# Sixteen small loads into an unread tile, set between the large loads of a one-core decode kernel

## The chip, the cores and the metric

One Trainium2 chip, one of its cores. The metric is the device time of one execution in microseconds; the kernel before has a median of 376.76 us over two runs (376.64 to 376.88). The profile is of one further execution of the same program, which took 376.91 us, of which 375.1 us lie between the first and the last recorded instruction.

## The reference

One token (a row `x` of 512 numbers) goes through a parallel block: attention over a cache of 4096 positions with 32 heads of 128, and beside it a gated feed-forward of width 1376. All is float32. Cut to what is computed:

```python
xn = layernorm(x)
q = (xn @ wq).reshape(1, 1, 32, 128).transpose(0, 2, 1, 3)
scores = einsum("bhqd,bhkd->bhqk", q, k_cache) * 128 ** -0.5
o = einsum("bhqk,bhkd->bhqd", softmax(scores), v_cache)
attn = o.transpose(0, 2, 1, 3).reshape(1, 1, 4096) @ wo
ffn = xn + ((silu(xn @ w_gate) * (xn @ w_up)) @ w_down) * sigmoid(xn @ w_r)
return x + attn + ffn
```

Two caches of 67.1 MB each and five weight matrices, about 159 MB in all, are read once from HBM and used once. (`silu` and `sigmoid` of the feed-forward act on one token; choosing the best of one token changes nothing.)

## The kernel before, in words

The 32 heads are worked in eight groups of four (`HP = 4`, `NG = 8`). For a group, `load_keys(g)` brings its keys as one load of 128 rows of 64 KB (8.39 MB) and `load_group(v_cache, g, ...)` its values as another load of that size; both are issued at line 102. Each row goes to one of the 128 partitions of the on-chip memory.

Two places hold these loads. `ring` has three slots of 32 KB a partition and some room behind; `vals` has two slots. The keys of group 0 go into `vals`, those of later groups into slots 0 and 1 or 1 and 2 of `ring` by turns; values go into `vals`, but those of the last group into `ring`. `wq` stands in the first two slots of `ring` at the start, `w_gate` and `w_up` in what lies behind them (four loads of 64 rows each, line 92, two for each matrix). At the end `w_down` (line 92, two loads) and `wo` (line 117, one load of 4096 KB and five of 2048, 1024, 640, 256 and 128 KB) go into places that have come free.

VectorE multiplies the keys with the query (line 250) and sums them (line 261); GpSimd takes a share of the rows (lines 266 and 268). TensorE forms the sum of the values with the softmax weights (line 338). A load into a place waits until the instructions that read the place before are done, and until the load that wrote it before has landed.

All these loads are issued by SyncE (rows of SPq) in the order of the program, and SyncE waits in that order too: an issue that must wait holds up all later ones. The order is `wq`, keys 0, `w_gate` twice, `w_up` twice, keys 1, values 0, keys 2, values 1 and so on to keys 7, values 6, values 7, `w_down`, `wo`. The rows `x` and `w_r` are issued by ScalarE. Loads that were issued stand in a queue at each of the 16 DMA engines, and an engine goes through its share of one after its share of the other. Eight semaphores serve the loads by turns to tell of landing; a load takes the semaphore of the load eight before it only once that one has landed.

After the last `wo` load, TensorE multiplies its rows (line 417), ScalarE and VectorE copy the row of results (lines 485 and 487), and SyncE stores it (line 488).

Of the kernel before, what the change touches and what calls it, by code (L numbers as in the profile page):

```python
# [8 lines left out]
F32 = mybir.dt.float32  # L9
# [4 lines left out]
P = 128  # L14
# [6 lines left out]
NCOL = 4  # L21
PARTS = (16,), (8, 4, 2.5, 1, 0.5)
T = 32


@with_exitstack
def kernel(
# [13 lines left out]
    nc = tc.nc  # L41
    _, H, Sk, Dh = k_cache.shape
# [26 lines left out]
    const = ctx.enter_context(tc.tile_pool(name="const", bufs=1))  # L69
# [12 lines left out]
    def load_wq(t):  # L82
        nc.sync.dma_start(t, wq.rearrange("(p j) n -> p (j n)", p=P))  # L83

        return [
            t[:, j * H * Dh:(j + 1) * H * Dh].rearrange("p (b h k n) -> p b h k n", b=NB, h=HP, n=QC)
            for j in range(NK)
        ]

    def halves(t, w):  # L90
        for i in range(2):
            nc.sync.dma_start(t[i::2], w[i::2])

    def load_in(t, w):
        halves(t, w.rearrange("(p j) f -> p (j f)", p=P))
        return [t[:, j * F:(j + 1) * F] for j in range(NK)]

    def load_group(cache, g, t, c0=0):

        n = t.shape[1]  # L100
        src = cache[0].rearrange("(b h g) (p c) d -> b g p h (c d)", b=NB, g=GB, p=PP)[g // GB, g % GB]
        nc.sync.dma_start(t, src[:, :, c0 * Dh:c0 * Dh + n])
        return t.rearrange("p (c d) -> p c d", d=Dh)

    def load_keys(g):

        i = (1 - g % 2) * SLOT
        t = load_group(k_cache, g, ring[:, i:i + 2 * SLOT] if g else vals)
        t = [t[:, :HC], t[:, HC:]]
        return [(h, t[h]) for h in ((1, 0) if g % 2 else (0, 1))]  # L110

    def load_wo(t, b, parts):
        src = wo[b * BH * Dh:(b + 1) * BH * Dh, :].rearrange("(p r) n -> p (r n)", p=P)
        x = 0
        for n in parts:
            y = x + int(n * D)
            nc.sync.dma_start(t[:, x:y], src[:, x:y])  # L117
            x = y
        return t.rearrange("p (r n) -> p r n", n=D)

    def load_down(t):
        halves(t, w_down.rearrange("f n -> (f n)").rearrange("(p x) -> p x", p=P))
        return t
# [4 lines left out]
    nc.scalar.dma_start(xr, x[0])  # L128
    nc.scalar.dma_start(wr, w_r.rearrange("(o n) -> o n", o=1))
    WQ = load_wq(ring[:, :2 * SLOT])  # L130
    K, V = {0: load_keys(0)}, {}


    ones = const.tile([P, P], F32, name="ones")
# [20 lines left out]

    own = const.tile([P, HP, T], F32, name="own")
    nc.vector.tensor_copy(own, mine[:, :, None].to_broadcast([P, HP, T]))

# [4 lines left out]

    first = const.tile([P, G, HP, T], F32, name="first")
    nc.gpsimd.memset(first, 0.0)
# [3 lines left out]
    for j in range(1, NCOL):  # L169
        nc.vector.tensor_tensor(sel, sel, rows_at[j], op=ALU.add)  # L170
    turned = const.tile([P, NCOL - 1 + T], F32, name="turned")
    nc.gpsimd.memset(turned, 0.0)
# [48 lines left out]
    for j in range(NK):  # L221
        for i in range(NQ * HP):
            t, k = i % NCOL, i // HP
            nc.tensor.matmul(ps_pv[i // NCOL][32 * t:32 * t + 1, :QC], xnT[:, j:j + 1],  # L224
                             WQ[j][:, k * QB // GB, i % HP, k % (GB // QB), :],
                             start=(j == 0), stop=(j == NK - 1), skip_group_check=True)
# [4 lines left out]

    behind = ring[:, 2 * SLOT:]
    W_GATE, W_UP = (load_in(behind[:, i * NK * F:(i + 1) * NK * F], w) for i, w in enumerate((w_gate, w_up)))
    late = [ring[:, SLOTS * SLOT + i * D:SLOTS * SLOT + (i + 1) * D] for i in range(MORE // D)]

    def q_part(k):

        ps = ps_q.tile([P, QB, Dh], F32, name="q")
        nc.tensor.matmul(ps.rearrange("p g d -> p (g d)"), pick.rearrange("p i h -> p (i h)"), q_sb[:, k, :],
                         start=True, stop=True)  # L240

        nc.scalar.activation(q_sb[:, k, :], ps.rearrange("p g d -> p (g d)"), AF.Copy)
        return ps
# [4 lines left out]
    def multiply(g, i, c0, c1):  # L248
        q, k = Q[g // QB][:, g % QB, :], K[g][i][1]
        nc.vector.tensor_tensor(  # L250
            k[:, c0:c1, :], k[:, c0:c1, :],
            q[:, None, :].to_broadcast([P, c1 - c0, Dh]), op=ALU.mult
        )

    def sums(g, i):
        if i == 0:
            S[g] = small.tile([P, C], F32, name="s")
        h, k = K[g][i]
        s = S[g][:, h * HC:(h + 1) * HC]
        for c, n in ((slice(0, HC - NP), Dh), (slice(HC - NP, HC), Dh // 2)):  # L260
            nc.vector.tensor_reduce(s[:, c], k[:, c, :n], axis=AX.X, op=ALU.add)  # L261

    def rest(g, i):

        k, q = K[g][i][1][:, HC - NP:], q_sb[:, g // QB, :].rearrange("p (g d) -> p g d", d=Dh)[:, g % QB, :]
        nc.gpsimd.tensor_tensor(k, k, q[:, None, :].to_broadcast([P, NP, Dh]), op=ALU.mult)  # L266
        a, b = k[:, :, :Dh // 2], k[:, :, Dh // 2:]
        nc.gpsimd.tensor_tensor(a, a, b, op=ALU.add)  # L268
# [17 lines left out]
    def ffn_hidden():  # L286

        hid = sigmoid(gate, [P, FT], "hid")
        nc.vector.tensor_tensor(hid, hid, gate, op=ALU.mult)
        hr = late[3][:, :(NS + 1) * T].rearrange("p (s i) -> p s i", i=T)  # L290
        nc.vector.memset(hr, 0.0)
        for a in range(HP):
# [5 lines left out]
            )  # L298
        hT = late[4][:, :(NS + 1) * T].rearrange("p (s i) -> p s i", i=T)
        nc.vector.transpose(hT.rearrange("p s i -> p (s i)"), hr.rearrange("p s i -> p (s i)"))  # L300
# [7 lines left out]
    def own_max(g):  # L308
        m = small.tile([P, 1], F32, name="m")
        nc.vector.reduce_max(m, S[g], axis=AX.X)  # L310
        dg = small.tile([P, PP], F32, name="dg")
        nc.vector.tensor_scalar(dg, fold, m, SCALE, op0=ALU.mult, op1=ALU.mult)  # L312
        ps = ps_s.tile([P, 512], F32, name="ps_small")
        nc.tensor.matmul(ps[:, :PP], same.rearrange("p i h -> p (i h)"), dg, start=True, stop=True)  # L314
        MX[g] = ps[:, :PP]

    def head_max(g):
        nm = small.tile([P, 1], F32, name="nm")
        nc.vector.tensor_reduce(nm, MX.pop(g), axis=AX.X, op=ALU.max, negate=True)  # L319
        MX[g] = nm  # L320

    def expo(g):
        nm, s = MX.pop(g), S.pop(g)
        if g % GB == 0:
            RS[g // GB] = small.tile([P, GB], F32, name="rs")
        e = small.tile([P, C], F32, name="e")
        nc.scalar.activation(e, s, AF.Exp, bias=nm, scale=SCALE, accum_out=RS[g // GB][:, g % GB:g % GB + 1])  # L327

        nc.gpsimd.tensor_tensor(PT[g % 2], e[:, :, None].to_broadcast([P, C, HP]),  # L329
                                mine[:, None, :].to_broadcast([P, C, HP]), op=ALU.mult)  # L330
# [90 lines left out]
    for g in range(NG + 1):  # L421
        if 0 < g < NG:
            K[g] = load_keys(g)
            V[g - 1] = load_group(v_cache, g - 1, vals)
        elif g:

            V[g - 1] = load_group(v_cache, g - 1, ring[:, SLOT:SLOTS * SLOT])

            WD = load_down(vals[:, :FP])
            WO = [load_wo(vals[:, SLOT:], 0, PARTS[0]), load_wo(ring[:, :SLOT], 1, PARTS[1])]  # L430
            acc = ps_q.tile([P, QB, Dh], F32, name="q").rearrange("p g d -> p (g d)")
            down = ps_q.tile([P, QB, Dh], F32, name="q").rearrange("p g d -> p (g d)")
            for t in (acc, down):
                nc.vector.memset(t, 0.0)
            nc.vector.tensor_copy(acc[0:1, :], base)
        if g:
            own_max(g - 1)
        n = (HC - NP) // 2
        if 0 < g < NG:
            rest(g, 0)  # L440
            multiply(g, 0, 0, n)
        if g:
            head_max(g - 1)
            expo(g - 1)
        if (g + 1) % QB == 0 and (g + 1) // QB < NQ:
            Q[(g + 1) // QB] = q_part((g + 1) // QB)
        if g < NG:
            rest(g, 1)
            if g:
                multiply(g, 0, n, HC - NP)  # L450
                sums(g, 0)
            multiply(g, 1, 0, HC - NP)
            sums(g, 1)
            if DEN:
                turn(*DEN.popitem())
        if g:
            values(g - 1)
            keep(g - 1)
            if g == 1:
                HL = ffn_hidden()  # L460
            if g == NG:
                sb = rows_down()
            if g % GB == 0:
                DEN[g // GB - 1] = collect(g // GB - 1)
# [4 lines left out]
    n = len(rows) - RB + PARTS[1][0]  # L469
# [47 lines left out]
```

## Time and profile before

| | |
|---|---|
| median of two runs | 376.76 us |
| the profiled execution | 376.91 us |
| its span, first to last instruction | 375.1 us |
| bytes read | 159.45 MB |
| packets | 3807 |
| VectorE busy | 228.0 us |
| GpSimd busy | 172.8 us |
| TensorE busy | 116.9 us |

Each load is cut into packets, one for each row, and ends on each engine that served it with a packet of a few bytes that tells of landing. A view of a stretch counts its packets by size and gives the time that they took as a share of the 16 engines' time in the stretch; so share times 16 times the length, over the count, is the mean time of one packet. A packet is counted with the stretch in which it starts, so the share of a short stretch can pass 100%.

### The profile page before, as it was taken

The numbers are of one execution on the slowest core, as the hardware profiler recorded it, in microseconds if no ns is written. First come the engines' busy times: TensorE is split into PE (matmuls) and PEld (weight loads), VectorE is DVE, ScalarE is ACT, GpSimd is POOL, SyncE is SP. The second block draws the span as 40 slices with busy tenths as digits, with TensorE's granted clock in tenths as the row PEclk, the third lists the DMA queues.
The fourth block names the chain that finished last, engine by engine and source line by source line (L and its number), as shares of the span: only waits on it lengthen the run. The fifth ranks groups of instructions, "written<-read, shape, count | busy, mean of one in ns | idle before, by whom it ended". The sixth has DMA issues, their size and how long they took to land.

```text
span 375.1 us, 2070 instructions
## 1 busy us (share of the span) xinstructions
PE 116.9 (31%) x848; PEld 34.0 (9%) x848; DVE 228.0 (61%) x130; ACT 16.1 (4%) x37; POOL 172.8 (46%) x60
## 2 busy tenths in 40 slices
PE   1155043000820073006300490036002600190985
PEld 1111010000200010001000130001000100020222
DVE  6300599289867990699059924995399419970020
ACT  3001000000010000100000000000000000000001
POOL 3000596089307940696059704980399019901000
PEclk9999566555675568556855597559555955575899
DMA  8999899999999999999999999999999999998995
GB/s 336 447 447 447 379 447 440 447 447 447 447 405 392 440 442 440 447 447 440 433 419 398 447 442 433 448 440 435 419 412 440 447 433 433 447 435 385 439 413 225
DMA packets 3807, 159.57 MB, mean 425 GB/s; under 512 B 468, under 2 KB 596, under 8 KB 855
## 3 DMA queue, kind: packets, MB, share of 16 engines
q1 hardware_dynamic: 3794, 159.45, 98.5%
q8 instruction: 6, 0.10, 0.1%
q14 instruction: 3, 0.02, 0.0%
q10 hardware_dynamic: 4, 0.00, 0.0%
HBM read 159.45 MB, written 0.00 MB: 425 GB/s over the span
## 4 chain that ended last, share of the span: by engine, by line
DMA 74%; PE 17%; DVE 7%; issue 0%; SPq 0%; ACTq 0%; ACT 0%; DVEq 0%
DMA vals<-in_A_v_cache_dram 55%; PE ps_pv L338 17%; DMA vals<-in_A_k_cache_dram 11%; DMA ring<-in_A_wo_dram 9%; DVE s L261 4%; DVE vals L250 3%; PE ps_acc L417 0%; SPq L117 0%; PE ps_small L314 0%; SPq L83 0%; ACTq L512 0%; ACT res L485 0%; DVE nm L319 0%; PE ps_o L417 0%; PE ps_pv L417 0%
## 5 line engine op out<-in xcount | busy, mean ns | idle before, releaser
L266 POOL TENSOR_TENSOR ring<-ring,q_sb 128x3072 f32<-128x3072 f32 x14 | 93.6, 6682 | 117.3 <-DMA ring<-in_A_k_cache_dram 117.3
L338 PE MATMUL ps_pv<-vals,pt 128*16 128x512 f32 x448 | 63.7, 733 | 189.5 <-DMA vals<-in_A_v_cache_dram 189.5
L250 DVE TENSOR_TENSOR ring<-ring,q 128x2560 f32<-128x2560 f32 (+1 forms) x21 | 77.8, 3704 | 71.6 <-DMA ring<-in_A_k_cache_dram 71.6
L261 DVE TENSOR_REDUCE s<-ring 128x40 f32<-128x5120 f32 (+1 forms) x28 | 100.0, 3615 | 0.8
L268 POOL TENSOR_TENSOR ring<-ring 128x1536 f32<-128x1536 f32 x14 | 48.1, 3436 | 1.1
L338 PEld LDWEIGHTS ps_pv<-vals,pt 128*16 128x16 f32 x448 | 15.2, 113 | 233.2 <-issue 233.2
L266 POOL TENSOR_TENSOR vals<-vals,q_sb 128x3072 f32<-128x3072 f32 x2 | 13.4, 6700 | 36.1 <-DMA vals<-in_A_k_cache_dram 36.1
L250 DVE TENSOR_TENSOR vals<-vals,q 128x5120 f32<-128x5120 f32 x2 | 11.0, 5484 | 27.6 <-DMA vals<-in_A_k_cache_dram 27.6
L261 DVE TENSOR_REDUCE s<-vals 128x40 f32<-128x5120 f32 (+1 forms) x4 | 14.3, 3615 | 0.1
L224 PE MATMUL ps_pv<-ring,xnT 128*1 128x512 f32 x64 | 10.0, 792 | 10.1 <-DMA ring<-in_A_wq_dram 10.1
L347 ACT ACTIVATE pv<-ps_pv 128x512 f32<-128x512 f32 x8 | 4.8, 597 | 192.2 <-PE ps_pv L338 192.2
L363 DVE RECIPROCAL rinv<-ps_small 128x4 f32<-128x4 f32 x2 | 0.4, 178 | 20.6 <-PE ps_small L354 20.6
L329 POOL TENSOR_TENSOR pt<-e,mine 128x512 f32<-128x512 f32 x8 | 8.3, 1040 | 8.9 <-ACT e L327 8.9
L338 PE MATMUL ps_pv<-ring,pt 128*16 128x512 f32 x64 | 8.5, 691 | 9.4 <-DMA ring<-in_A_v_cache_dram 9.4
L275 PE MATMUL ps_acc<-ring,xnT 128*1 128x344 f32 x32 | 4.3, 717 | 15.0 <-DMA ring<-in_B_w_gate_dram 15.0
L327 ACT ACTIVATE e<-s,nm 128x128 f32<-128x128 f32 x8 | 3.2, 402 | 119.6 <-DVE nm L319 119.6
L314 PE MATMUL ps_small<-dg,same 128*128 128x32 f32 x16 | 3.6, 310 | 14.9 <-DVE dg L312 14.9
L356 PE MATMUL ps_o<-pv,first 128*128 128x512 f32 x16 | 7.4, 604 | 0.4 <-ACT pv L347 0.4
L268 POOL TENSOR_TENSOR vals<-vals 128x1536 f32<-128x1536 f32 x2 | 6.9, 3444 | 0.2
L275 PE MATMUL ps_o<-ring,xnT 128*1 128x344 f32 x32 | 3.8, 631 | 3.7 <-DMA ring<-in_B_w_up_dram 3.7
L314 PEld LDWEIGHTS ps_small<-dg,same 128*128 128x128 f32 x16 | 2.9, 219 | 21.2 <-issue 12.0
L195 PE MATMUL ps_small<-ones,pv 1*128 1x1 f32 x8 | 2.0, 370 | 8.3 <-DVE pv L191 8.3
(102 smaller groups left out, 80.3 us busy)
## 6 DMA issues: line engine op xcount, KB each, us to landing
vals<-in_A_wo_dram SPq DMA_DIRECT2D x1, 4096.0 KB, 25.7
ring<-in_B_w_gate_dram SPq DMA_DIRECT2D x2, 1376.0 KB, 44.7
ring<-in_B_w_up_dram SPq DMA_DIRECT2D x2, 1376.0 KB, 48.6
vals<-in_B_w_down_dram SPq DMA_DIRECT2D x2, 1376.0 KB
ring<-in_A_wo_dram SPq DMA_DIRECT2D x1, 2048.0 KB
ring<-in_A_wo_dram SPq DMA_DIRECT2D x1, 1024.0 KB, 32.1
ring<-in_A_wo_dram SPq DMA_DIRECT2D x1, 640.0 KB, 33.2
ring<-in_A_wo_dram SPq DMA_DIRECT2D x1, 256.0 KB, 33.4
```

Of the source, the lines that this page charges most:

```text
L224: nc.tensor.matmul(ps_pv[i // NCOL][32 * t:32 * t + 1, :QC], xnT[:, j:j + 1], WQ[j][:, k * QB // GB, i % HP, k % (GB // QB), :], start=(j ...
L250: nc.vector.tensor_tensor(k[:, c0:c1, :], k[:, c0:c1, :], q[:, None, :].to_broadcast([P, c1 - c0, Dh]), op=ALU.mult)
L261: nc.vector.tensor_reduce(s[:, c], k[:, c, :n], axis=AX.X, op=ALU.add)
L266: nc.gpsimd.tensor_tensor(k, k, q[:, None, :].to_broadcast([P, NP, Dh]), op=ALU.mult)
L268: nc.gpsimd.tensor_tensor(a, a, b, op=ALU.add)
L275: nc.tensor.matmul(ps[32 * t:32 * t + 1, :FT], xnT[:, j:j + 1], W[j][:, t * FT:(t + 1) * FT], start=(j == 0), stop=(j == NK - 1), skip_gro ...
L314: nc.tensor.matmul(ps[:, :PP], same.rearrange("p i h -> p (i h)"), dg, start=True, stop=True)
L327: nc.scalar.activation(e, s, AF.Exp, bias=nm, scale=SCALE, accum_out=RS[g // GB][:, g % GB:g % GB + 1])
L329: nc.gpsimd.tensor_tensor(PT[g % 2], e[:, :, None].to_broadcast([P, C, HP]), mine[:, None, :].to_broadcast([P, C, HP]), op=ALU.mult)
L338: nc.tensor.matmul(ps[r:r + M, :], p[:, G * i:G * (i + 1), :].rearrange("p c h -> p (c h)"), v[:, G * i:G * (i + 1), :].rearrange("p c d - ...
L347: nc.scalar.activation(PV[g // GB][:, :, g % GB, :], ps_pv[g % 2].rearrange("p (c d) -> p c d", c=G), AF.Copy)
L356: nc.tensor.matmul(ps_o, first[:, c].rearrange("p h i -> p (h i)"), pv[:, c].rearrange("p k d -> p (k d)"), start=(c == 0), stop=(c == G - 1))
```

## The change

A tile `marks` of 128 by 128 numbers is added, and a function `mark(n)`, which loads the first `n` rows (512 bytes each) of the key cache of head 0 into the first `n` partitions of that tile. Nothing reads the tile. `mark` is called sixteen times: after keys 0, after the second load of `w_up`, and then after the issue of each of keys 1 to 7 and of values 0 to 6. It takes 15, 14, 13, 12 and 11 rows by turns, and 16 the last time; together that is 211 rows, 108 KB. No call stands behind values 7, `w_down` or `wo`. All sixteen write the same partitions of one tile, and all are issued by SyncE.

```diff
+MARKS = (15, 14, 13, 12, 11, 15, 14, 13, 12, 11, 15, 14, 13, 12, 11, 16)
...
     WQ = load_wq(ring[:, :2 * SLOT])
+    marks = const.tile([P, Dh], F32, name="marks")
+
+    def mark(n):
+        nc.sync.dma_start(marks[:n], k_cache[0, 0, :n, :])
+
     K, V = {0: load_keys(0)}, {}
+    mark(MARKS[0])
...
     W_GATE, W_UP = (load_in(behind[:, i * NK * F:(i + 1) * NK * F], w) for i, w in enumerate((w_gate, w_up)))
+    mark(MARKS[1])
...
         if 0 < g < NG:
             K[g] = load_keys(g)
+            mark(MARKS[2 * g])
             V[g - 1] = load_group(v_cache, g - 1, vals)
+            mark(MARKS[2 * g + 1])
```

## Rows read from the trace of the kernel before

**Rows 1.** The page: the busy share of the 16 DMA engines in 40 equal slices of the span, in tenths, what they moved, and the count of packets by size.
```profile
DMA  8999899999999999999999999999999999998995
GB/s 336 447 447 447 379 447 440 447 447 447 447 405 392 440 442 440 447 447 440 433 419 398 447 442 433 448 440 435 419 412 440 447 433 433 447 435 385 439 413 225
DMA packets 3807, 159.57 MB, mean 425 GB/s; under 512 B 468, under 2 KB 596, under 8 KB 855
```

**Rows 2.** The page: DMA queues, with packets, MB and share of the 16 engines' time over the span.
```profile
q1 hardware_dynamic: 3794, 159.45, 98.5%
q8 instruction: 6, 0.10, 0.1%
q14 instruction: 3, 0.02, 0.0%
```

**Rows 3.** Busy time of each engine by stretches of time (us from the start of the span): length, busy us of PE, PEld, DVE, ACT and POOL with their counts of instructions, granted clock, share of the DMA engines, GB/s.
```profile
50.00:100.00 50.00, 12.07 (x84) 3.15 (x78) 41.66 (x15) 0.49 (x2) 33.52 (x8) 0.57 1.00 434
150.00:200.00 50.00, 8.76 (x66) 2.37 (x66) 34.04 (x14) 2.07 (x6) 29.26 (x7) 0.60 1.01 439
300.00:350.00 50.00, 13.51 (x86) 3.46 (x90) 27.45 (x14) 1.59 (x5) 22.24 (x6) 0.59 0.99 428
350.00:371.00 21.00, 18.52 (x184) 5.97 (x176) 2.20 (x4) 1.79 (x3) 0.00 (x0) 1.00 0.97 414
371.00:375.10 4.10, 1.43 (x36) 0.69 (x32) 0.56 (x2) 0.54 (x2) 0.00 (x0) 1.00 0.07 25
```

**Rows 4.** The chain of waits in order of time, its end: start us, us, what.
```profile
338.13 33.21 DMA ring<-in_A_wo_dram
371.34 0.04 issue
...
372.51 0.27 ACT res L485
```

**Rows 5.** DMA packets of the stretch from 60 to 66 us: counts by size, and the queue's packets, MB and share.
```profile
DMA packets 33, 2.16 MB, mean 360 GB/s; under 512 B 0, under 2 KB 0, under 8 KB 0
q1 hardware_dynamic: 33, 2.16, 83.1%
```

**Rows 6.** The same from 371.7 to 372.2 us, in the last load of 128 rows of 1 KB.
```profile
DMA packets 18, 0.02 MB, mean 31 GB/s; under 512 B 3, under 2 KB 18, under 8 KB 18
q1 hardware_dynamic: 18, 0.02, 9.0%
```

**Rows 7.** The same from 371.9 to 372.3 us.
```profile
DMA packets 5, 0.00 MB, mean 8 GB/s; under 512 B 2, under 2 KB 5, under 8 KB 5
q1 hardware_dynamic: 5, 0.00, 2.4%
```

**Rows 8.** The page's DMA issues: engine, operation, count, KB of each, median us from issue to landing.
```profile
ring<-in_B_w_up_dram SPq DMA_DIRECT2D x2, 1376.0 KB, 48.6
ring<-in_A_wo_dram SPq DMA_DIRECT2D x1, 640.0 KB, 33.2
ring<-in_A_wo_dram SPq DMA_DIRECT2D x1, 256.0 KB, 33.4
```

**Rows 9.** The same view, the loads whose size the page leaves out (8.39 MB each) and the last 128 KB.
```profile
ring<-in_A_wo_dram SPq DMA_DIRECT2D x1, 128.0 KB, 25.9
ring<-in_A_k_cache_dram SPq DMA_DIRECT2D x7, 25.7
vals<-in_A_v_cache_dram SPq DMA_DIRECT2D x7, 29.1
vals<-in_A_k_cache_dram SPq DMA_DIRECT2D x1, 40.7
```

**Rows 10.** SyncE's issues in order of time: start us, us, line, load, count.
```profile
1.18 0.62 SPq L102 DMA_DIRECT2D vals<-in_A_k_cache_dram  x1
3.20 1.25 SPq L92 DMA_DIRECT2D ring<-in_B_w_up_dram  x2
32.67 0.55 SPq L102 DMA_DIRECT2D ring<-in_A_k_cache_dram  x1
127.36 0.54 SPq L102 DMA_DIRECT2D ring<-in_A_k_cache_dram  x1
142.94 0.54 SPq L102 DMA_DIRECT2D vals<-in_A_v_cache_dram  x1
166.05 0.53 SPq L102 DMA_DIRECT2D ring<-in_A_k_cache_dram  x1
181.03 0.54 SPq L102 DMA_DIRECT2D vals<-in_A_v_cache_dram  x1
373.13 0.31 SPq L488 DMA_DIRECT2D out_dram<-res  x1
```

**Rows 11.** The same view, the stretches from 338.5 and from 346 us alone (the third and fourth piece of `wo` into `ring`, and the fifth).
```profile
338.13 0.91 SPq L117 DMA_DIRECT2D ring<-in_A_wo_dram  x2
346.36 0.33 SPq L117 DMA_DIRECT2D ring<-in_A_wo_dram  x1
```

**Rows 12.** What SyncE waited for: line, releaser, us in total, times, longest us.
```profile
SPq L117 <- DMA ring<-in_A_v_cache_dram: 7.3, 1, 7.3
SPq L512 <- DMA out_dram<-res: 0.6, 1, 0.6
```

**Rows 13.** TensorE in order of time, from 40 to 60 us: start us, us, operation, and in brackets the idle time before and what ended it.
```profile
56.70 3.75 PE L275 MATMUL ps_o<-ring,xnT 128*1 128x344 f32 x31 [3.68 <-DMA ring<-in_B_w_up_dram]
```

## The prediction

> **What bounds the kernel now.** I read the slices of the page first, then the queues, then the stretches, then the end of the chain. In the slices the DMA engines stand at 9 tenths all the way, and the bandwidth sits between 379 and 447 GB/s from the second slice to the last but one [rows 1]. The queue of SyncE's loads alone fills 98.5% of the 16 engines' time [rows 2]. The stretches say the same: 1.00, 1.01 and 0.99 of the DMA engines' time, while no compute engine passes 42 of 50 us [rows 3]. So the queue never runs empty between the first load and the last, and the time is the sum of the packets on an engine. The end agrees: the chain goes over a `wo` load that lands at 371.34, and 1.2 us later the row of results is copied [rows 4]; what follows 371 moves almost nothing, at 0.07 of the DMA engines [rows 3].
>
> The prices of packets come from stretches in which the queue holds one kind. Between 60 and 66 us 33 packets of 64 KB take 83.1% of 96 us of engine time, 2.417 us each [rows 5]. In the last load, of 1 KB rows, two stretches give two equations for a, the 1 KB packet, and b, the packet of a few bytes that ends a load: 15a + 3b = 9.0% of 8 us = 0.72 us [rows 6], and 3a + 2b = 2.4% of 6.4 us = 0.154 us [rows 7]; so a is 46.6 ns and b 7 ns. A floor follows too: 159.45 MB [rows 2] over 16 engines is 152 packets of 64 KB for each, 367.5 us.
>
> **The change, part by part.** It adds 16 loads and 211 rows, and takes away or moves nothing in the code; it does hold SyncE up, which comes below.
>
> *The packets.* An added load ends up in the same 16 queues, behind a large load. A row is 512 bytes, a size that the trace does not show. Between 1 KB at 46.6 ns and 64 KB at 2417 ns the line has 37.6 ns for each KB and 9 ns at zero; at half a KB it gives 28 ns. With the closing packet of 7 ns that is 35 ns for each engine and added load. From below the price is the closing packet alone, 7 ns; from above a full 1 KB packet and the close, 54 ns. I take 35, on the line that also passes near b.
>
> *How many engines pay.* Packets under 512 bytes number 468 [rows 1]. The 29 SyncE loads of many rows, with 16 closing packets each, make 464, and the three transfers of one row (`x`, `w_r`, the result) one each make 467; one more is the program's own. So a load of one row is closed on one engine, one of 64 or 128 rows on sixteen; for 11 to 16 rows I take one engine for each row. [...] I take the most that one engine can be asked to pay, sixteen, for the engine that ends last: 16 x 35 ns = 0.56 us. The ends of this term are one closing packet, 0.01 us, and 16 x 54 ns = 0.86 us.
>
> *The boundary between loads.* I cost it at nothing beyond its packets. The pieces of `wo` show it: issued at 338.13 and about 338.61, the 640 KB and 256 KB pieces land 33.2 and 33.4 us later, at 371.3 and 372.0, and the 128 KB piece, issued at 346.36, 25.9 us later, at 372.3 [rows 8, 9, 11]. So the last two come 0.7 and 0.3 us after the one before. For the last, eight packets of 46.6 ns and a close are 0.38 us. Nothing is left for a start or a drain between two loads whose successor is already queued.
>
> *SyncE's issues.* An issue costs SyncE 0.3 to 0.6 us [rows 10, 11], sixteen together some 6 us, and SyncE waits most of the time anyway. All rows go to one tile, so each added load must wait until the one before has landed, and what is queued behind it on SyncE is the next large load. Nobody but SyncE waits for it. In the steady part: keys issued at 127.36 land 25.7 us later, near 153.1 [rows 9, 10]. The added load behind values of 142.94 waits for the one behind those keys, until about 153; the next keys are due at 166.05, 13 us of slack. The one behind those keys waits for the values of 142.94, which land 29.1 us later, at 172.0; the next values are due at 181.03, 9 us of slack. So the large issues keep their times.
>
> *The one place where a large issue does move* is the start. The first added load lands behind keys 0, at 1.18 + 40.7 = 41.9 us [rows 9, 10]; the second waits for it, behind `w_up`, and keys 1, now issued at 32.67 [rows 10], wait behind that on SyncE until 43 or so. The cover is `w_gate` and `w_up`: the first half of `w_up` lands at 3.20 + 48.6 = 51.8 [rows 8, 10], and TensorE starts on the second at 56.70 by its landing [rows 13]. The queue holds work for some 9 to 13 us more; if the first added load landed later than that after keys 0, the queue would run empty.
>
> *The semaphores.* The last piece of `wo` waited 7.3 us for values 7, which touch none of its bytes [rows 12]; that is the reuse of a semaphore, eight loads on. The added loads double the turns before, so a large load waits for one four large loads back instead of eight, long landed; behind values 7 none is added, and this wait stays. Nothing.
>
> **The sum.** Own time of the profiled execution 376.91 + 0.56 = 377.47 us. The median of the runs shown stands 0.15 us below that execution, so I predict 377.3 us, 0.15% up.
>
> **The rivals.**
>
> *A drain at each small load (slower).* If the queue of an engine stood still until a small load had landed, the price would be the time of such a load alone: the store of the result, 2 KB, is issued at 373.13, and the end waits for it for 0.6 us after an issue of 0.31 us [rows 10, 12]; about 1.2 us to the end of that wait, with the short instructions between. Sixteen are 19 us, 396 us in all. It decides from 0.47 us a load on, since 16 x 0.47 = 7.5 us is 2%. Against it stands the 0.3 us between the last two pieces of `wo`, in which no 1.2 us fits. [...] Chance 4%.
>
> *A small bubble at each small load.* Reads of half a KB may leave part of a latency open that eight rows in succession hide. At 0.1 to 0.45 us each, 1.6 to 7 us: 378.5 to 384 us. For it is only that the trace has no load of one small packet for an engine amid large ones. Chance 7%.
>
> *One more fetch of instructions.* SyncE gets more instructions. The six fetches of 16 KB take 0.1% of 6000 us of engine time, about 1 us each [rows 2]; one more, on the engine that ends last, gives 378.3. Chance 7%.
>
> *The loads do not run*, being read by nothing: 376.8 us, chance 2%. A gain beyond 2% has no room: the packets need 367.5 us, 371 lands the last, and the copy and store stay. I leave it 1%.
>
> **How the numbers follow.** The forecast has 79%, with its own range from 376.7 (0.01 us more, less the scatter of 0.1) to 377.8 (0.86 us, and the same scatter). The range from 376.5 to 379.0 us takes in the fetch of instructions and the lower part of the bubbles, and a scatter of some tenths to the low side. A measurement of this kernel tells 2% from no change, 369.2 to 384.3 us: the forecast, the bubbles, the fetch and the loads that do not run are within, 95%; the drain is slower, 4%; faster 1%.
>
> **What would show it.** In the changed profile: packets up by about 422 (211 rows and 211 closes) and 0.1 MB; the queue's share still above 98%; keys 1 issued near 43 instead of 32.67, and the later large issues within 1 us of theirs; waits of SyncE on `marks` of some 10 us each, with none of the engines' waits for keys or values longer than before by more than that 1 us. Wrong would be a gap in the DMA slices, above all near 55 us, or stretches at 1.00 that fall to 0.97: then the boundary or SyncE's order has a price that the rows of before hide.

## The result and the profile after

The changed kernel took 381.07 and 383.82 us in its two executions, a median of 382.44 us against 376.76 us. The ratio to the kernel before is 1.0149, with a 95% interval from 1.012 to 1.0179. The prediction was 377.3 us, with a range up to 379.0: the time moved, by 5.7 us instead of half a microsecond, and the range does not hold it. (Ratios given here leave out executions more than 1.5% above the fastest of the same kernel; where the scatter is itself the finding, all executions are given.)

The profile is of the execution of 381.07 us. First the page: the span, the slices, the packets and the main queue. They answer to [rows 1, 2].

```profile
span 379.3 us, 2087 instructions
DMA  8999998999999999999989999999999999998995
GB/s 332 442 442 442 406 502 387 409 442 443 442 437 442 443 430 436 360 422 436 435 374 435 443 444 422 443 443 423 443 435 443 401 429 435 416 403 386 454 403 231
DMA packets 4228, 159.68 MB, mean 421 GB/s; under 512 B 678, under 2 KB 1017, under 8 KB 1276
q1 hardware_dynamic: 4216, 159.56, 98.5%
```

Three things are to be seen. The 421 more packets are the 211 rows and their closes, as forecast (one of the program's own packets is missing). The queue's share is 98.5% as before, so it never ran dry. But the slice at 152 us (the seventeenth) moved 360 GB/s instead of 447, and others fell too, though a slice of 9.5 us catches packets unevenly. So the time was not lost between packets; the stretches below show that it was lost in them.

The stretches show it. These are rows of the view by stretches, with the columns of [rows 3]; the last two columns are the share of the DMA engines and the GB/s.

```profile
157.00:171.00 14.00, 0.00 (x0) 0.00 (x0) 13.90 (x4) 0.03 (x1) 13.90 (x4) 0.50 0.98 379
310.00:326.00 16.00, 0.00 (x0) 0.00 (x0) 15.64 (x6) 0.49 (x2) 15.56 (x4) 0.50 1.01 438
331.00:337.00 6.00, 6.00 (x44) 1.40 (x40) 5.84 (x5) 0.00 (x0) 0.71 (x1) 0.69 1.00 371
```

The share is the same in all three, the bandwidth is not: 379 and 371 against 438. A packet that takes longer kept its engine just as busy (0.98 and 1.00 against 1.01). What does tell is the mean time of a packet of 64 KB, by the same division as in [rows 5]. The view of DMA packets, for the stretches 158 to 164, 176 to 182, 331 to 337 and 343 to 346 us:

```profile
q1 hardware_dynamic: 32, 2.10, 90.5%
...
q1 hardware_dynamic: 34, 2.23, 85.6%
...
q1 hardware_dynamic: 34, 2.23, 99.6%
...
q1 hardware_dynamic: 18, 1.18, 90.7%
```

90.5% of 96 us over 32 packets is 2.715 us; then 85.6% of 96 over 34, 2.417 us; then 99.6% of 96 over 34, 2.81 us; then 90.7% of 48 over 18, 2.419 us. The price of before was 2.417 us. So values 2, from about 151 to 173 us, ran 12% slow from end to end, eight packets of 0.30 us more on each engine, 2.4 us. Values 7 ran 16% slow from 327 to 339 us, four packets of 0.4 us, 1.6 us. With half a microsecond for the added packets that is 4.5 us, against a span longer by 379.3 - 375.1 = 4.2 us.

SyncE did what was forecast. Its waits, from the view of waits, and its issues:

```profile
SPq L135 <- DMA marks<-in_A_k_cache_dram: 156.6, 15, 37.1
...
SPq L118 <- DMA ring<-in_A_v_cache_dram: 8.9, 1, 8.9
```

```profile
42.58 0.55 SPq L103 DMA_DIRECT2D ring<-in_A_k_cache_dram  x1
...
165.96 0.53 SPq L103 DMA_DIRECT2D ring<-in_A_k_cache_dram  x1
174.81 0.30 SPq L135 DMA_DIRECT2D marks<-in_A_k_cache_dram  x1
183.27 0.54 SPq L103 DMA_DIRECT2D vals<-in_A_v_cache_dram  x1
```

Fifteen waits on `marks` take 156.6 us, 10.4 each; keys 1 are issued at 42.58; the keys due at 166.05 [rows 10] come at 165.96. The first issue to come more than a microsecond late stands behind the slow values 2, 183.27 against 181.03, and those after it keep about that lag.

### The profile page after: what moved, and what is told of

The parts are those of the page before. It is cut to its first block, busy times and chain, and to the rows that moved or that the text cites. A ratio compares the mean times of both kernels' runs of the same rounds, so it can differ in the third digit from the quotient of the medians.

```text
span 379.3 us, 2087 instructions
## 1 busy us (share of the span) xinstructions
PE 117.0 (31%) x848; PEld 33.8 (9%) x848; DVE 228.0 (60%) x130; ACT 16.1 (4%) x37; POOL 172.8 (46%) x60
## 3 DMA queue, kind: packets, MB, share of 16 engines
q1 hardware_dynamic: 4216, 159.56, 98.5%
## 4 chain that ended last, share of the span: by engine, by line
DMA 75%; PE 17%; DVE 7%; issue 0%; SPq 0%; ACTq 0%; ACT 0%; DVEq 0%
DMA vals<-in_A_v_cache_dram 55%; PE ps_pv L346 16%; DMA vals<-in_A_k_cache_dram 11%; DMA ring<-in_A_wo_dram 9%; DVE s L269 4%; DVE vals L258 3%; PE ps_acc L425 0%; SPq L118 0%; PE ps_small L322 0%; SPq L84 0%; ACTq L522 0%; ACT res L495 0%; DVE nm L327 0%; PE ps_o L425 0%; PE ps_pv L425 0%
## 5 line engine op out<-in xcount | busy, mean ns | idle before, releaser
L346 PE MATMUL ps_pv<-vals,pt 128*16 128x512 f32 x448 | 62.4, 719 | 192.9 <-DMA vals<-in_A_v_cache_dram 192.9
L346 PE MATMUL ps_pv<-ring,pt 128*16 128x512 f32 x64 | 9.3, 745 | 11.0 <-DMA ring<-in_A_v_cache_dram 11.0
L231 PE MATMUL ps_pv<-ring,xnT 128*1 128x512 f32 x64 | 9.2, 738 | 10.6 <-DMA ring<-in_A_wq_dram 10.6
L283 PE MATMUL ps_o<-ring,xnT 128*1 128x344 f32 x32 | 4.8, 771 | 2.4 <-DMA ring<-in_B_w_up_dram 2.4
```

Of the source, the lines that this page charges most:

```text
L283: nc.tensor.matmul(ps[32 * t:32 * t + 1, :FT], xnT[:, j:j + 1], W[j][:, t * FT:(t + 1) * FT], start=(j == 0), stop=(j == NK - 1), skip_gro ...
L346: nc.tensor.matmul(ps[r:r + M, :], p[:, G * i:G * (i + 1), :].rearrange("p c h -> p (c h)"), v[:, G * i:G * (i + 1), :].rearrange("p c d - ...
```

## The experiments

Edits are shown against the changed kernel; where only lines with + stand, each takes the place of that kernel's line of the same kind, and ... marks what is left out. Before the first runs four theories stood. **S**: the unequal counts of rows shift the 16 engines against each other, and some alignments slow all. **D**: a disturbance from outside. **P**: any small load slows the large one behind it. **H**: holding SyncE back does it. All runs here were timed beside the kernel before, whose medians were 376.78 to 377.07 us and whose executions, 97 in all, lay between 376.67 and 377.28 us.

### The changed kernel again

> The changed kernel once more. In its profile the packets cost what was predicted (27 ns for a row of 512 bytes), but 64 KB packets took 2.71 us instead of 2.42 from 151 to 172 us and 2.82 us from 327 to 337 us. Theory S (the unequal counts of rows shift the 16 engines against each other, and some alignments of their reads slow all of them for a load or two): the stretches return, 379 to 384 us, not at the same place in each run. Theory D (a disturbance from outside the kernel in those two executions): most executions at 377.3 us, and the kernel before shows such stretches too. Theory P (a small load slows the large load behind it): 379 to 384 us. Theory H (holding SyncE back does it): 379 to 384 us.

Seven executions from 377.83 to 387.54 us, median 383.10; ratio 1.0101 (1.0065 to 1.0137). Theory D falls: the 18 executions of the kernel before on the same chip stayed within 376.67 to 377.18. The scatter of ten microseconds is a property of the changed kernel, and the interval worked out from its first two executions was narrower than that scatter. In the profile the slow stretches lie elsewhere: here 142 to 150 us, 46 packets in 103.0% of 128 us, 2.87 us each.

```profile
q1 hardware_dynamic: 46, 3.01, 103.0%
```

### Sixteen rows each time, and eight

```diff
-MARKS = (15, 14, 13, 12, 11, 15, 14, 13, 12, 11, 15, 14, 13, 12, 11, 16)
+MARKS = (16,) * 16
```

> All sixteen added loads have 16 rows, so each engine that serves them gets the same. Theory S: no shift between engines beyond that of the kernel before, 377.3 us (0.56 us over the kernel before), no stretch of slow packets. Theory D: 377.3 us. Theory P and theory H: as the changed kernel, 379 to 384 us.

```diff
+MARKS = (8,) * 16
```

> All sixteen added loads have 8 rows, so at most eight engines get them and run 0.56 us behind the others by the end, from packets alone. Theory S: a shift larger than in the changed kernel between two halves, so slow stretches, 378.5 us or more. Theory D: 377.3 us. Theory P: 379 us or more. Theory H: 379 us or more.

With 16 rows: 402.39 to 422.37 us in six executions, median 413.55. With 8 rows: 376.65 to 377.24 us in eleven, ratio 1.0005 (0.9996 to 1.0014). Theory S fails on both sides: equal counts for all engines are far the worst, and counts that shift half of the engines are harmless. Theory P fails on the eight rows, and so does theory H, for these loads hold SyncE in the same way. Its waits with 8 rows are 151.4 us, where the changed kernel's were 156.6:

```profile
SPq L135 <- DMA marks<-in_A_k_cache_dram: 151.4, 15, 37.1
```

With 16 rows the packets of 76 to 92 us and of 134 to 139 us are these:

```profile
q1 hardware_dynamic: 110, 7.21, 103.9%
...
q1 hardware_dynamic: 31, 2.03, 111.0%
```

103.9% of 256 us over 110 is 2.418 us, and 111.0% of 80 us over 31 is 2.86 us. Behind the first four added loads nothing is slow: 432 GB/s at a share of 1.00 from 92.9 to 112.2 us. Behind the fifth the page's slices of 10 us still hold 420 and 419 GB/s, from 110 to 130 us. Behind the sixth, near 131 us, it is 371 GB/s at a share of 1.01, from 131.7 to 154.4 us.

### The same rows without holding SyncE

```diff
-    marks = const.tile([P, Dh], F32, name="marks")
+    marks = [const.tile([P, Dh], F32, name=f"marks{i}") for i in range(4)]
     def mark(n):
-        nc.sync.dma_start(marks[:n], k_cache[0, 0, :n, :])
+        marks.append(marks.pop(0))
+        nc.sync.dma_start(marks[-1][:n], k_cache[0, 0, :n, :])
```

> The rows of the changed kernel, but into four tiles by turns, so that an added load waits for the one four before and SyncE is hardly held. Keys 1 are issued near 33 us again. Theory H: 377.3 us and no slow stretch. Theory S and theory P: 379 to 384 us. Theory D: 377.3 us.

377.79 to 389.69 us in six executions, median 381.44: as the changed kernel. Keys 1 are issued at 31.78 us again:

```profile
31.78 0.55 SPq L103 DMA_DIRECT2D ring<-in_A_k_cache_dram  x1
41.97 0.31 SPq L136 DMA_DIRECT2D marks<-in_A_k_cache_dram  x1
```

Theory H falls for good. What was left was what distinguishes 16 rows from 8: the rows that are read, the places that are written, the number of engines.

### Rows far apart, places far apart, all partitions, nine rows

```diff
+MARKS = (16,) * 16
...
-        nc.sync.dma_start(marks[:n], k_cache[0, 0, :n, :])
+        nc.sync.dma_start(marks[:n], k_cache[0, 0, ::Sk // n, :])
```

> Sixteen loads of 16 rows, the rows 256 apart in the key cache (128 KB from one to the next) instead of one behind the other. With 16 rows side by side the time was 402 to 422 us, and whole large loads ran at 2.71 to 2.97 us a packet; with 8 rows none did. Theory R (sixteen engines read the same 8 KB at almost one time, lose their order there, and the next load keeps the bad order): 377.4 us, no slow load. Theory W (the 16 rows are written to partitions 0 to 15, where engines get in each other's way): 395 us or more, as with rows side by side. Theory N (any added load that reaches more than eight engines draws the engines' order anew): 395 us or more.

```diff
+MARKS = (16,) * 16
...
-        nc.sync.dma_start(marks[:n], k_cache[0, 0, :n, :])
+        nc.sync.dma_start(marks[::P // n], k_cache[0, 0, :n, :])
```

> Sixteen loads of 16 rows side by side in the key cache, but written to partitions 0, 8, 16 and so on to 120 instead of 0 to 15. Theory W: 377.4 us, no slow load. Theory R and theory N: 395 us or more.

```diff
+MARKS = (128,) * 16
```

> Sixteen loads of 128 rows of 512 bytes, so each engine takes eight rows of the load, as it does of a large one. Own cost 8 x 27 + 9 ns = 0.225 us a load, 3.6 us in all. Theory W: 380.4 us, no slow load, since each engine writes its own partitions. [...] Theory N: 395 us or more.

```diff
+MARKS = (9,) * 16
```

> Sixteen loads of 9 rows. With 8 rows 377.0 us, with 11 to 16 by turns 378 to 390 us, with 16 402 to 422 us. If a bound lies between eight engines and nine (theory N, and theory W if it is the upper engines that disturb), slow loads return: 378.5 us or more. If the loss grows with the number of rows (theory R), 377.1 to 378 us.

| 16 added loads of | executions | range, us | median, us |
|---|---|---|---|
| 16 rows 128 KB apart, to partitions 0 to 15 | 4 | 397.22 to 419.38 | 417.24 |
| 16 rows side by side, to partitions 0, 8, ... 120 | 10 | 377.16 to 377.75 | 377.42 |
| 128 rows, to all partitions | 4 | 379.80 to 380.08 | 379.96 |
| 9 rows, to partitions 0 to 8 | 10 | 376.94 to 377.55 | 377.16 |

Theory R falls, theory N falls, theory W stands: what counts is where the 16 rows are written, not which are read. These runs also measure the price that the prediction had worked out. With 16 rows spread out, 377.42 - 376.93 = 0.49 us (ratio 1.0014, 1.0005 to 1.0024), where 0.56 was the sum. With 128 rows, 379.96 - 376.93 = 3.03 us, 0.19 us a load, where eight rows at 27 ns and a close at 9 ns, as the changed kernel's trace records them, make 0.225. In the run with the rows spread, packets keep their price from 157 to 165 us: 94.5% of 128 us over 50, 2.42 us.

```profile
q1 hardware_dynamic: 50, 3.28, 94.5%
```

### Crossing the middle, or crowding

If the engines take the 128 rows of a large load in order, which no view here shows, its upper eight engines write to partitions 64 to 127, and rows 8 to 15 of an added load take these engines to the other half. So two explanations of theory W stood: an engine leaves its half of the partitions (C), or many engines write to a few neighbours at once (K).

```diff
+MARKS = (16,) * 16
...
-        nc.sync.dma_start(marks[:n], k_cache[0, 0, :n, :])
+        nc.sync.dma_start(marks[56:56 + n], k_cache[0, 0, :n, :])
```

> Sixteen loads of 16 rows side by side, written to partitions 56 to 71 instead of 0 to 15: just as crowded, but the first eight rows lie below partition 64 and the last eight from 64 on. Theory C (a large load's first eight engines write below partition 64 and its last eight from 64 on; an added row that makes an engine write in the other half draws the engines' alignment anew, and the next large loads may run slow): 377.4 us and no slow load, for no engine changes its half. Theory K (the crowding of 16 rows on few neighbouring partitions): 395 us or more, as with partitions 0 to 15.

```diff
+MARKS = (8,) * 16
...
+        nc.sync.dma_start(marks[64:64 + n], k_cache[0, 0, :n, :])
```

> Sixteen loads of 8 rows written to partitions 64 to 71 instead of 0 to 7. With 0 to 7 it was 377.0 us. Theory C: the first eight engines now write in the other half, so slow loads and 385 us or more. Theory K: 8 rows on neighbouring partitions, 377.0 us as before.

```diff
+        nc.sync.dma_start(marks[:8 * n:8], k_cache[0, 0, :n, :])
```

> The changed kernel with its counts by turns (15, 14, 13, 12, 11 and 16 last), but row r goes to partition 8r instead of r. Theory C: no row crosses, 377.3 us, the sum of the prediction, and no slow load. Theory S (unequal counts shift the engines against each other): 379 to 384 us as in the changed kernel.

Sixteen rows at 56 to 71: 403.07 to 425.62 us in four executions. Eight rows at 64 to 71: 376.95 to 377.50 us in ten. The changed kernel's own counts by turns, but with row r at partition 8r: 377.10 to 378.71 us in ten, median 377.38, ratio 1.0015 (1.0006 to 1.0024). Theory C falls on both of the first two runs, and theory S once more on the third. The packets of the run at 56 to 71 reach the slowest rate shown here, between 357 and 365 us: 90.3% of 128 us over 38, 3.04 us.

```profile
q1 hardware_dynamic: 38, 2.49, 90.3%
```

Crowding stands, and the changed kernel with its rows spread is the kernel that the prediction described.

One more run puts 16 rows 4 partitions apart, on 0 to 60, one another 12 rows on 0 to 11.

```diff
+MARKS = (16,) * 16
...
+        nc.sync.dma_start(marks[:4 * n:4], k_cache[0, 0, :n, :])
```

> Sixteen loads of 16 rows side by side in the cache, written to partitions 0, 4, 8 and so on to 60. Rows 8 apart over all 128 partitions (8r) cost 377.4 us; side by side at 0 to 15 and at 56 to 71 they cost 402 us and more. Crowding (many engines write to a few neighbouring partitions at once): 377.4 us, since no two engines write to neighbouring partitions. If it is the share of the 128 partitions that is reached (half of them here): slow loads, 385 us or more.

```diff
+MARKS = (12,) * 16
```

> Sixteen loads of 12 rows to partitions 0 to 11. With 9 rows 377.2 us, with 11 to 16 by turns 378 to 390, with 16 397 to 422 us. If the loss grows with the number of crowded rows: between 378 and 395 us, with some slow loads in the profile. If only 13 rows and more disturb: 377.3 us.

Four partitions apart: eleven executions, nine from 377.25 to 377.75 us and two at 378.65 and 379.47, median 377.33, so reaching only half of the partitions does no such harm. The profile is of the execution of 379.47 us: the packets of 160 to 168 us take 90.7% of 128 us over 48, 2.42 us. In its chain a load of `wo` is issued at 338.07 us, as before (338.13 us [rows 4]), but lands 35.75 us later instead of 33.21. So what that execution lost shows only behind that issue, and its cause stays open.

```profile
q1 hardware_dynamic: 48, 3.15, 90.7%
...
338.07 35.75 DMA ring<-in_A_wo_dram
```

Twelve rows: 377.08 to 378.67 us in ten, median 377.47. The profiled one took 377.45 us, 0.55 us over the median of the kernel before (376.90), about the price of the packets, which leaves no room for a large load that runs slow from end to end (2.4 us in the changed kernel). So on neighbouring partitions 9 rows cost nothing clear of noise; 12 cost about their packets and a microsecond more now and then, as the rows 4 apart do too; 16 cost some 37 us. The 12 rows fell below the 378 us that growth with the rows was given, and at two executions above the 377.3 of the other expectation; neither fits.

### How long it lasts

```diff
-MARKS = (15, 14, 13, 12, 11, 15, 14, 13, 12, 11, 15, 14, 13, 12, 11, 16)
+MARKS = (0, 0, 0, 0, 0, 16, 0, 0, 0, 0, 0, 0, 0, 0, 0, 0)
...
+        if n:
+            nc.sync.dma_start(marks[:n], k_cache[0, 0, :n, :])
```

> A single added load, of 16 rows to partitions 0 to 15, behind values 1 (it runs near 131 us); the other fifteen are left out. If a bad alignment lasts until something disturbs the engines again, one load of 8 KB can slow several large loads: some executions 377, others 379 to 390 us, and in the profile of a slow one the rate changes near 131 us and changes back only near a fetch of instructions (139, 216, 242 us), not at the border of a load. If an added load slows only the load right behind it: 376.8 to 380 us, and one load of 2.7 to 2.9 us a packet at most.

One crowded load at this place: 376.74 to 377.25 us in eleven executions, nothing.

```diff
+MARKS = (0, 0, 0, 0, 0, 16, 0, 0, 0, 0, 0, 0, 0, 0, 0, 0)
...
+    marks = [const.tile([P, Dh], F32, name=f"marks{i}") for i in range(4)]
...
+        for t in marks if n else ():
+            nc.sync.dma_start(t[:n], k_cache[0, 0, :n, :])
```

> Four loads of 16 rows to partitions 0 to 15, one right behind the other after values 1 (near 131 us), into four tiles so that none waits; nothing at the other places. One such load at this place made no difference (376.96 us), sixteen at sixteen places made the first slow load near 131 us, 112 us or 230 us. If small shifts of the engines against each other add up over several crowded loads until a bad alignment is reached, and it lasts until the next disturbance: 377.1 us in some executions, 379 to 395 us in others, with more than one large load slow and changes of rate near 131 us and near the fetches of instructions. If shifts do not add up: 377.1 us in all.

Four in a row at the same place: ten executions from 377.08 to 377.78 us and one of 390.09. A large load at 3.04 us a packet, the slowest rate shown above, loses 8 x 0.62 = 5.0 us; 13 us are more than one such load would lose. One in eleven is thin support for shifts that add up, and no more than that. That execution has no profile, so a kernel with the first ten of the crowded loads, and none behind values 3, was run:

```diff
+MARKS = (16,) * 10 + (0,) * 6
...
+        if n:
+            nc.sync.dma_start(marks[:n], k_cache[0, 0, :n, :])
```

> The first ten of the sixteen loads of 16 rows to partitions 0 to 15, up to the one behind values 3 (near 210 us); the last six are left out. If a bad alignment lasts until the next disturbance: after about 210 us the rate of the packets stays as the last added load left it, over the borders of large loads, and changes only near fetches of instructions (about 216 to 225, 243 to 255, 260 to 275, 335 to 355 us); 380 to 415 us. If a slow load ends with its own border: 2.42 us a packet from the second large load after 210 us on, and less than 400 us.

388.23 to 406.09 us in four executions. In the profile the last added load runs between 230 and 233 us. The view of DMA packets of five stretches behind it, 244 to 252, 252 to 257, 256 to 264, 268 to 270 and 280 to 288 us:

```profile
q1 hardware_dynamic: 46, 3.01, 106.6%
...
DMA packets 38, 1.44 MB, mean 288 GB/s; under 512 B 16, under 2 KB 16, under 8 KB 16
...
DMA packets 46, 2.95 MB, mean 369 GB/s; under 512 B 1, under 2 KB 1, under 8 KB 1
q1 hardware_dynamic: 46, 2.95, 104.3%
...
q14 instruction: 1, 0.01, 1.2%
...
q1 hardware_dynamic: 51, 3.34, 96.3%
```

106.6% of 128 us over 46 is 2.966 us a packet. Then a large load ends: 16 closes, and no row of 512 bytes among the packets. Then 104.3% of 128 us over 45 large packets: 2.967 us, the same to a thousandth, on the other side of the border. Near 269 us one engine serves a fetch of instructions, and from there on it is 96.3% of 128 us over 51, 2.417 us. So the slow rate outlives the load that brought it, crosses the border of large loads, and here ended beside a fetch on one engine. In the changed kernel the slow stretch of values 7 ended likewise, between 338 and 340 us:

```profile
q8 instruction: 1, 0.02, 3.5%
```

These are two returns to 2.42 us beside a fetch. The slow stretch of values 2 in the changed kernel ended without one, at an added load: 2.71 us a packet from 166 to 170 us, 11 rows of 512 bytes and no fetch from 172 to 174 us, 2.42 us from 176 to 182 us. Nor does every fetch end a slow stretch: in the run with ten crowded loads the packets took 2.966 us from 212 to 220 us and again from 244 to 252 us, with a fetch between 238 and 241 us. No run took the fetches away, so this is a coincidence in time and not yet a cause. And in the second profile of the changed kernel one slow stretch began near 287 us with neither an added load nor a fetch beside it (109.6% of 128 us over 58, 2.42 us, from 277 to 285 us; 89.1% of 48 us over 16, 2.67 us, from 289 to 292 us).

## Why the prediction was wrong

- **What bounds the kernel** held: the 16 engines' queues stay full, before and after (98.5%).
- **The packets** held: 16 x 35 ns = 0.56 us was the sum, and 0.43 us (377.38 against 376.95) and 0.49 us were measured where no load is slow. The trace of the changed kernel records 27 ns for a row and 9 ns for a close: one of each take 5.6% of 640 ns from 41.56 to 41.60 us, 36 ns, a row and two closes 7.0% from 174.00 to 174.04 us, 45 ns. One engine for each row held as well: the queue's packets went from 3794 to 4216, 211 rows and 211 closes. That the engine that ends last pays all sixteen times was my choice; no view names an engine.
- **SyncE's issues**, the start and the semaphores held, by the issues and waits shown above, and by the runs that hold SyncE in the same way (8 rows) or hardly at all (four tiles).
- **The boundary between loads is the step that failed.** I cost it at nothing beyond its packets and took the pieces of `wo` as witness [rows 8, 9, 11]. They are loads of 128 rows to 128 partitions, with 16 closes each, so eight rows for an engine on the mean. The added loads put up to 16 engines on up to 16 neighbouring partitions. With 128 rows the step is right (380 us by packets alone); in the changed kernel it is wrong by 5 to 6 us, and with 16 rows at 0 to 15 by some 36 us. I had bounded the size of the packet from both sides, but not the place that it is written to.
- **The rate of the large packets** was taken as fixed at 2.417 us. It is the lowest of the means shown here, but not fixed: 2.42, 2.71, 2.81, 2.87, 2.97 and 3.04 us were seen among others, and a mean can hold for long (2.71 us in each 4 us from 154 to 170 us in the changed kernel).
- **The rivals.** The time fell among the small bubbles, 378.5 to 384 us, for which I gave 7%. That is chance, for their mechanism is not what happened: where no large load is slow a small one costs no more than its packets (377.0 us with 8 rows, 377.4 us with 16 rows spread), while some of the crowded ones turn whole large loads slow, and the executions scatter over ten microseconds. The drain, the fetch and the loads that do not run are excluded by the profile.
- **What would show it.** I named a stretch whose share falls from 1.00 to 0.97. The share stayed; the GB/s and the mean time of a packet were the signs.

## What to carry to other kernels

Between large loads a small load may cost more than its own bytes. Here it did when 16 rows went to neighbouring partitions, so there are two things to try: send its rows to partitions spread over the memory (row r to 8r cost half a microsecond for sixteen loads of 16 rows, row r to r some 20 to 46), or keep it to eight rows. When a queue is full and the kernel still loses time, divide share by packets: a busy share of 100% hid packets that had become 12 to 26% slower. And where executions suddenly scatter over ten microseconds beside a neighbour that repeats within 0.6 us, one profile is a sample.

## What the runs showed that was not expected

Loads of 8 KB can slow the 8.39 MB loads behind them by 12 to 26%, and sixteen of them, on neighbouring partitions, cost 20 to 49 us (397 to 426 us). Where the rows are written was changed by itself, so that it decides is shown; the number of engines and the number of rows in a load went up together, so which of the two makes the crowd is not. The slow rate can hold over tens of microseconds (2.966, 2.966 and 2.967 us a packet from 212 to 220, 244 to 252 and 256 to 264 us), took several values up to 3.04 us, and began behind a crowded load though not behind the first ones: behind the sixth with 16 rows at 0 to 15 (above), the fifth with 16 at 56 to 71 (2.42 us from 96 to 110 us, 2.71 from 116 to 130), the eleventh with the rows 128 KB apart (2.43 us from 212 to 227 us, 2.71 from 233 to 239), the fourth with ten crowded loads (2.42 us from 76 to 92 us, 2.92 from 97 to 112). The one exception shown is that near 287 us. Of the three ends shown, two lie beside a fetch and one at an added load. That small shifts of the engines against each other add up until their accesses collide is how I read this; that the shifts are the cause was not shown, only that two slow stretches end beside a fetch on one engine.

What it is in the place that decides was not shown. With 16 rows it was 397 to 426 us at 0 to 15 and at 56 to 71, and 377.4 and 377.3 us in the median 8 and 4 partitions apart; 8 rows at 0 to 7 and at 64 to 71 cost nothing clear of noise (377.0 and 377.2 us). Whether the large loads, while they run slow, collide where HBM is read or where the partitions are written stays open.
